# Masks of the exponentials for 54 later attention tiles: from VectorE's fused compare-and-multiply to a GpSimd addition and ScalarE's row sums

## The chip, the cores and the metric

One core of one Trainium2 chip. Its engines run their own instruction streams side by side and wait for each other through semaphores: TensorE (PE in the rows, its weight loads PEld), VectorE (DVE), ScalarE (ACT), GpSimd (POOL), and SyncE (SP), which here only issues DMAs. The metric is the device time of one execution in microseconds (us); lower is better.

## What is computed

Top-k attention, and behind it a mixture of experts with one expert a row. Eight batches of eight heads, 576 positions, 64 columns a head; every row of scores keeps its 32 largest values:

```python
scores = scale * np.matmul(q, k.transpose(0, 1, 3, 2))
kth = np.partition(scores, -top_k, axis=-1)[..., -top_k:-top_k + 1]
mask = scores >= kth
scores = np.where(mask, scores, -1000000000.0)
scores = scores - np.max(scores, axis=-1, keepdims=True)
attn = np.exp(scores)
attn = attn / (np.sum(attn, axis=-1, keepdims=True) + 1e-09)
return np.matmul(attn, v)
# then: x = rows of all heads side by side (4608 x 512), 8 experts
logits = x @ w_gate + modality_bias[modality_id]
e_idx = np.argmax(logits, axis=1)
h = np.maximum(x[mask] @ w1[e], 0.0)        # 512 -> 1024
out[mask] = gate_w[mask, None] * (h @ w2[e])  # 1024 -> 512
```

## The kernel before

The scores are cut into 288 tiles of 128 rows by 576 columns: nine for each of the 32 pairs of heads, 36 for each batch. One Python loop of 310 steps writes all engines' instructions; step i works on a different stage of each of about a dozen tiles, so that a tile u passes through the steps u-2 to u+9. The order inside a step is fixed by the code, except on VectorE, where `arrange` sorts the step's operations by given weights and puts the masking operation last.

What happens to tile u, with the step and the engine:

- u-2: the scores on PE (`qk`, L410) and their copy to SBUF on ACT (`sevac`, L420: tile `Ssb`, ten buffers).
- u, u+1: the largest values of six pieces of the row (`cand`, L427) and their merging (`mg`, L438 to L440) on DVE: the first 24 values.
- u+3: signs against the 24th value on ACT (`K`, L460). u+4: `y` = scores times signs on POOL (`pool_y`, L466), so that only the values under the 24th stay positive. u+5: the next eight of them on DVE (`find`, L470), and, at every third tile, the 32nd value `kth` of three tiles (`pick`, L477 to L479).
- u+6: the exponential of the whole tile on ACT (`expo`, L484: `ex`, three buffers). u+7: `keep` (L490) on DVE compares with `kth`, multiplies, writes `P` and sums the rows. u+8: `gate` (L562), one element of `P` read on POOL, which holds POOL until the masking is done.
- u+9: the transposes of `P` on PE (L577), their copy on ACT (L585, `PT`), and behind that the products with v (L605).

For tiles under 48 that are not the third of three there is another way, already in the kernel before (`early`; in the first batch without the tiles of `wide`, below): at u+7 `hide` (L497) on DVE writes -2^100 where a score is under `kth` and 0 elsewhere, in bf16; at u+8 `hidden` (L503) on POOL adds it to the scores (`z`, in a buffer of `ex`), and at the end of ACT's step u+8 `masked` (L558) takes the exponential of `z`, writes `P` and sums the rows in the same instruction. `expo`, `keep` and `gate` are then left out. Four of nine tiles under 36 go a third way (`wide`), which the change doesn't touch. The third tile of three (u % 3 = 2) always goes through `keep`.

Beside this the experts' products fill PE (`moe`, a queue of operations, L883 and L896; each of weight 0.88 is one product of 128x512 or two of 128x256). Every step gives PE a budget, `STEP` = 3.36, from which the attention's own costs are taken; what is left over, up to a cap, is spent on the queue. Results of the experts leave by indirect DMAs that POOL issues (L911, two for a slot of 256 rows), at most one in a step, behind `y`. What the queue still holds when the loop ends is done before the remaining slots, which are computed in three products each for precision (L1127, L1156, L1172). These names of the planner matter to the change: `side`, `rush`, `chore`, `posted` and `sends` hold the work of routing and of planning slots, `moe` the experts' operations.

Of the kernel before, what the change touches and what calls it, by code (L numbers as in the profile page):

```python
# [11 lines left out]
BF = mybir.dt.bfloat16  # L12
# [9 lines left out]
CAP = 2.6  # L22
# [8 lines left out]
STEP = 3.36  # L31
# [10 lines left out]
LR = LT + 2  # L42
LE = LR - 1
TL = LR + 2
# [21 lines left out]
END = (-3, 1.0)  # L66
SP_ = (0, 0, 0, 0, 0)
HUGE = float(2.0 ** 100)
EARLY = 48
WIDE = 36  # L70
BIG = float(2.0 ** 80)
MAX_TOP = 64.0
# [7 lines left out]
def kernel(  # L80
# [14 lines left out]
    B, H, S, D = q.shape  # L95
# [4 lines left out]
    NT = NPAIR * 9  # L100
# [111 lines left out]
    hT = const.tile([128, FC, SLOT], FT, name="hT")  # L212
# [31 lines left out]
    V.tensor_scalar(idw, idf, BIG * (1.0 + 2.0 ** -7), None, op0=OP.mult)  # L244
    tops = const.tile([128, WIDE], FT, name="tops")
    tiny = flat(w2b)[:, 2 * S + 448:2 * S + 576].bitcast(BF)
# [4 lines left out]
    zr = const.tile([128, XW], FT, name="zr")  # L251
# [123 lines left out]
    role = lambda i: (i - 1) % 9  # L375
    wide = lambda i: main[0] and i < WIDE and role(i) < 4

# [64 lines left out]
    def small(i0):  # L442
        on = main[0] and i0 < WIDE
        s = tops[:, i0:i0 + 3] if main[0] and i0 < WIDE else wk.tile([128, 3], FT, name="sm", bufs=6)
        for x in range(3):
            T[i0 + x]["s"] = s
        G.tensor_scalar(s, T[i0]["mg"][:, :, 0], -1.0, 0.0 if on else 1.0, op0=OP.mult, op1=OP.min if on else OP.mult)
# [33 lines left out]
    def expo(i):  # L481
        t = T[i]
        t["ex"] = wk.tile([128, S], FT, name="ex", bufs=XB)
        A.activation(t["ex"], t["S"], AF.Exp, bias=t["s"][:, i % 3:i % 3 + 1])  # L484
# [7 lines left out]
    def hide(i):  # L492

        t = T[i]
        x = 2 * (i % 2)
        t["hb"] = hT[:, x:x + 2, :].rearrange("p f t -> p (f t)").bitcast(BF)[:, :S]
        V.tensor_scalar(t["hb"], t["S"], kth[:, i:i + 1], -HUGE, op0=OP.is_lt, op1=OP.mult)  # L497

    def hidden(i):
# [229 lines left out]
    chore = deque()  # L729
# [214 lines left out]
    side = deque()  # L944
    rush = deque()
    moe = deque()
    sends = deque()
    puts = deque()
    posted = deque()
# [114 lines left out]
    def bounds():  # L1064
# [3 lines left out]
        V.tensor_scalar(bt, kth, KTH_MAX, 0.0, op0=OP.is_ge, op1=OP.add, accum_out=bd_[:, 1:2])  # L1068
        V.tensor_scalar(bt[:, :WIDE], tops, -MAX_TOP, 0.0, op0=OP.is_le, op1=OP.add, accum_out=bd_[:, 2:3])

    def beyond():

        bb = bd_.bitcast(BF)[:, 8:11]
        V.tensor_scalar(bb, bd_[:, 0:3], 0.0, None, op0=OP.is_gt)
        pbad = psX.tile([128, 3], FT, name="X")
        PE.matmul(pbad, onesb, bb, start=True, stop=True)
        V.tensor_reduce(bd_[:, 3:4], pbad, axis=AX.X, op=OP.add)
        V.tensor_copy(badi, bd_[0:1, 3:4])
# [16 lines left out]
            keep_warm(KP)  # L1095
        sevac(x)
    ok = lambda x: 0 <= x < NT
    early = lambda u: wide(u) or u < EARLY and u % 3 != 2
    dn_of = lambda u: den[(u // 36) % 2][:, (u // 9) % HP, role(u):role(u) + 1]
    PREP, PREP0 = dict(zip(PJ, "tkq")), dict(zip(PJ0, "tkq"))  # L1100
    two = lambda nm, shape: [wk.tile(shape, FR, name=nm + x) for x in "hl"]
# [88 lines left out]
    spare_pe = 0.0  # L1190
# [19 lines left out]
    for i in range(LAST):  # L1210
# [5 lines left out]
        cost = COST["trans"] * ok(i - TL)  # L1216
        p, j = divmod(i, 9)
        u = i - TL
# [14 lines left out]
        u = i - (KL + 1)  # L1233
# [4 lines left out]
        while after:  # L1238
            after.popleft()()
        u = i - LE  # L1240
        if ok(u) and not early(u):
            expo(u)
        while nxt:
# [3 lines left out]
        u = i - TL  # L1247
        if ok(u):
            evac(u)
        u = i - LR - 1  # L1250
# [59 lines left out]
        u = i - (TL + 1)  # L1310
        if avs:
            c, f = avs.popleft()
            f()
            cost += c
        if ok(u) and role(u) in (3, 7, 8):
            f = av(u // 9, role(u), xTs(u // 36)[(u // 9) % HP])
# [12 lines left out]
            bounds()  # L1329
        if i == NT + LR + 4:  # L1330
            beyond()
        spare_pe = min(spare_pe + (STEP if i < NT + TL + END[0] else END[1]) - cost, CAP)
        while seen[0] and spare_pe > 0:
            if i < NT + ME and not alone[0]:
                more_moe()
# [2 lines left out]
            c, f, new = moe[0]  # L1338
# [31 lines left out]
        for x in range((RNQ if quick else RN) if rush else 0):  # L1370
            f = rush.popleft() if rush else PAUSE
# [6 lines left out]
        for x in range((SNQ if quick else SN) - len(small_)):  # L1378
            f = side.popleft() if side and not rush else PAUSE
# [6 lines left out]
        if ok(i - LR):  # L1386
            u = i - LR
            end.append(Op("keep", lambda: hide_wide(u) if wide(u) else hide(u) if early(u) else keep(u, dn_of(u)), got, *cut_))
# [192 lines left out]
```

## Time and profile before

| | us |
|---|---|
| median of 3 runs (1189.47 to 1190.32) | 1189.72 |
| the profiled execution | 1187.03 |
| its span, first to last instruction | 1185.4 |
| busy in the span: PE, DVE | 1154.1, 1085.2 |
| busy in the span: ACT, POOL | 971.7, 662.2 |
| granted TensorE clock, mean | 0.993 |

The attention fills the span to about 1010 us, the slots in three products the rest. Busy times count an instruction from its start to its end; on PE and DVE instructions overlap in a pipeline, so that the distance between the starts of two neighbours says more of the pace than the length of one. In a list in order of time the columns are start, length, engine, line, operation, tiles written and read, and in brackets the idle time ahead of it with what ended it.

### The profile page before, as it was taken

The page shows a single profiled execution, that of the slowest core. Times are in us where ns is not written, and L with a number is a line of the kernel's source. Part 1 is how long each engine was busy: PE and PEld are TensorE (multiplying, and loading weights), DVE is VectorE, ACT ScalarE, POOL GpSimd, SP SyncE. Part 2 cuts the span into 40 slices and gives each one's busy share as a digit, 9 for nine tenths or more (in the row PEclk, how much of TensorE's full clock was granted, in tenths as well). Part 3 has the DMA queues.
Part 4 walks back from the last instruction along what each step waited for, and adds up shares of the span by engine and source line. Part 5 has one row for each costly group of instructions (what it writes and reads, how often), then busy time and mean ns, then how long its engine had stood idle before and what let it go on. Part 6 is the DMA issues. An engine that isn't in the chain of part 4 may idle for free.

```text
span 1185.4 us, 28210 instructions
## 1 busy us (share of the span) xinstructions
PE 1154.1 (97%) x7998; PEld 908.1 (77%) x7998; DVE 1085.2 (92%) x5473; ACT 971.7 (82%) x1995; POOL 662.2 (56%) x1281
## 2 busy tenths in 40 slices
PE   8999989999999999999999999999999999999998
PEld 6777768687777868778686878778687777589987
DVE  7999999999999999999999899999999998476762
ACT  5988969998999889998999899989999887355653
POOL 6888875565556465566656566557655655221111
PEclk9999989999999999999999999999999999999999
DMA  5664468653677367665786458564765554287750
GB/s 123 161 187 90 89 183 228 191 134 97 168 222 210 83 174 229 166 152 129 217 228 176 109 151 250 155 166 128 201 188 133 176 139 153 73 287 245 249 191 22
DMA packets 204325, 197.11 MB, mean 166 GB/s; under 512 B 104414, under 2 KB 151534, under 8 KB 204161
## 3 DMA queue, kind: packets, MB, share of 16 engines
q1 hardware_dynamic: 196880, 175.92, 54.6%
q0 software_dynamic: 6080, 19.00, 4.5%
q8 instruction: 67, 1.10, 0.4%
q14 instruction: 98, 0.79, 0.2%
q10 hardware_dynamic: 1200, 0.30, 0.1%
HBM read 118.63 MB, written 24.23 MB: 121 GB/s over the span
## 4 chain that ended last, share of the span: by engine, by line
PE 48%; DVE 43%; ACT 4%; issue 2%; POOL 1%; DMA 1%; SPq 0%; POOLq 0%; ACTq 0%; DVEq 0%
DVE cand L427 12%; PE E L883 8%; DVE mg L470 8%; PE E L896 8%; PE X L605 7%; DVE P L490 7%; PE S L410 5%; PE X L1172 5%; PE T L577 5%; PE X L1156 4%; DVE cand L438 2%; DVE cand L439 2%; DVE mg L440 2%; DVE mg L438 2%; PE E L1156 1%
## 5 line engine op out<-in xcount | busy, mean ns | idle before, releaser
L427 DVE MAX8 cand<-Ssb 128x8 f32<-128x96 f32 x1632 | 366.8, 244 | 1.4 <-ACT Ssb L420 1.4
L466 POOL TENSOR_TENSOR y<-Ssb,K 128x576 f32<-128x576 f32 x272 | 347.1, 1276 | 7.1 <-ACT K L460 6.8
L410 PE MATMUL S<-ks,qs 128*128 128x288 f32 x992 | 222.7, 346 | 8.2 <-ACT Ssb L420 5.1
L460 ACT ACTIVATE K<-Ssb,n 128x576 bf16<-128x576 f32 x272 | 216.6, 796 | 8.8 <-POOL y L466 8.4
L470 DVE MAX8 mg<-y 128x8 f32<-128x576 f32 x288 | 213.1, 740 | 3.9 <-POOL y L466 3.9
L420 ACT ACTIVATE Ssb<-S 128x576 f32<-128x576 f32 x270 | 178.2, 660 | 44.8 <-PE S L410 32.2
L883 PE MATMUL E<-xgT,w1b 128*128 128x256 f32 x832 | 201.4, 384 | 2.6 <-ACT hT L887 1.6
L585 ACT ACTIVATE PT<-T 128x640 f32<-128x640 f32 (+1 forms) x288 | 192.8, 669 | 11.3 <-PE T L577 6.9
L896 PE MATMUL E<-w2b,hT 128*128 128x512 f32 x416 | 195.9, 597 | 0.5 <-ACT hT L887 0.2
L410 PEld LDWEIGHTS S<-ks,qs 128*128 128x128 f32 x992 | 152.9, 190 | 53.8 <-issue 30.0
L484 ACT ACTIVATE ex<-Ssb,sm 128x576 f32<-128x576 f32 x244 | 193.4, 793 | 0.0
L490 DVE SCALAR_TENSOR_TENSOR P<-Ssb,kth,ex 128x576 f32<-128x576 f32 x226 | 185.8, 822 | 3.1 <-ACT ex L484 1.7
L883 PEld LDWEIGHTS E<-xgT,w1b 128*128 128x128 f32 x832 | 150.8, 190 | 29.3 <-ACT hT L887 6.8
L562 POOL TENSOR_SCALAR spare<-P 1x1 f32<-1x1 f32 x226 | 40.8, 180 | 217.1 <-DVE mg L438 180.4
L577 PE MATMUL T<-idf,P 128*128 128x128 f32 x1080 | 157.8, 273 | 1.3 <-ACT PT L585 0.7
L605 PE MATMUL X<-PT,vm 128*64 128x256 f32 (+1 forms) x1536 | 146.6, 333 | 1.0 <-ACT xgT L842 0.5
L577 PEld LDWEIGHTS T<-idf,P 128*128 128x128 f32 x1080 | 130.2, 141 | 4.0 <-ACT PT L585 1.9
L605 PEld LDWEIGHTS X<-PT,vm 128*64 128x64 f32 x1536 | 88.2, 137 | 45.7 <-issue 11.0
L896 PEld LDWEIGHTS E<-w2b,hT 128*128 128x128 f32 x416 | 72.7, 190 | 59.6 <-issue 55.0
L453 POOL TENSOR_SCALAR n<-mg 128x1 f32<-128x1 f32 x288 | 63.2, 219 | 97.2 <-DVE mg L440 80.2
L1178 POOL DMA_INDIRECT out_dram<-ot,tk x12 | 12.1, 1012 | 90.9 <-ACT ot L1177 90.9
L460 ACT ACTIVATION_READ_ACCUMULATOR K<-Ssb,n 128x1 f32 x272 | 59.9, 220 | 0.0
(273 smaller groups left out, 2253.2 us busy)
## 6 DMA issues: line engine op xcount, KB each, us to landing
w1b<-in_moe_w_dram SPq DMA_DIRECT2D x76, 512.0 KB
w2b<-in_moe_w_dram SPq DMA_DIRECT2D x76, 512.0 KB
ks<-st SPq DMA_DIRECT2D x62, 288.0 KB
ks<-st SPq DMA_DIRECT2D x62, 256.0 KB
qs<-st SPq DMA_DIRECT2D x124, 128.0 KB
xg<-xs SPq DMA_DIRECT2D x19, 516.0 KB
vm<-in_v_dram SPq DMA_DIRECT2D x32, 256.0 KB
km<-in_k_dram SPq DMA_DIRECT2D x63, 128.0 KB
```

What stands on the lines that cost most here:

```text
L410: PE.matmul(ps[:, hf, :288], l, m, start=(n == 0), stop=(n == len(terms) - 1))
L427: return [lambda s=s: V.max(c[:, s * 8:s * 8 + 8], T[i]["S"][:, bnd[s]:bnd[s + 1]]) for s in range(NSUB)]
L460: A.activation(t["K"], t["S"], AF.Sign, scale=2.0 ** -24 - 1.0, bias=t["n"][:, 1, i % 3:i % 3 + 1], accum_out=t["n"][:, 0, i % 3:i % 3 + 1])
L466: G.tensor_tensor(t["y"], t["S"], t["K"], op=OP.mult)
L470: V.max(t["mg"][:, i % 3, 24:32], t["y"])
L484: A.activation(t["ex"], t["S"], AF.Exp, bias=t["s"][:, i % 3:i % 3 + 1])
L490: V.scalar_tensor_tensor(t["P"], t["S"], kth[:, i:i + 1], t["ex"], op0=OP.is_ge, op1=OP.mult, accum_out=dn)
L577: PE.transpose(T[i]["pt"][:, x, :], (Pm if c == 4 else Pb[c % 2])[:, h * 512 + x * 128:h * 512 + x * 128 + 128], idf)
L585: A.activation(o, T[i]["pt"][:, :n], AF.Exp if wide(i) else AF.Copy)
L605: PE.matmul(o.rearrange("p (a b) -> p a b", a=2) if j < 8 else o, l, r, start=(c == 0), stop=(c == 4))
L883: PE.matmul(ps[:, f % 2], w1b[:, c, f * 128:(f + 1) * 128], xgT[:, c, :], start=(c == 0), stop=(c == KC - 1))
L896: PE.matmul(o["py"], hT[:, f, t * 128:(t + 1) * 128], w2b[:, f, :], start=(f == 0), stop=(f == FC - 1))
```

## The change

In the steps r = 15 to 32 of a batch's 36 (`CALM`, counted from the batch's end behind the pipeline), where none of the routing and planning queues holds work and the experts' queue holds 3 to 24 operations, a tile from 48 on that isn't the third of three goes the way of `hide`, `hidden` and `masked`. The tile's mask lies in `zr`, one buffer for all of them. In the step in which such a tile is masked the experts' budget is smaller by 0.22 (`DROP`).

```diff
+CALM = (15, 33)
+DROP = 0.22
...
-        t["hb"] = hT[:, x:x + 2, :].rearrange("p f t -> p (f t)").bitcast(BF)[:, :S]
+        if i < EARLY:
+            t["hb"] = hT[:, x:x + 2, :].rearrange("p f t -> p (f t)").bitcast(BF)[:, :S]
+        else:
+            t["hb"] = zr.bitcast(BF)[:, :S]
         V.tensor_scalar(t["hb"], t["S"], kth[:, i:i + 1], -HUGE, op0=OP.is_lt, op1=OP.mult)
...
-    early = lambda u: wide(u) or u < EARLY and u % 3 != 2
+    calm = set()
+    early = lambda u: wide(u) or u < EARLY and u % 3 != 2 or u in calm
...
         u = i - LE
+        if (ok(u) and u >= EARLY and u % 3 != 2 and CALM[0] <= (i - TL - 2) % 36 < CALM[1] and 3 <= len(moe) <= 24
+                and not any((side, rush, chore, posted, sends))):
+            calm.add(u)
         if ok(u) and not early(u):
             expo(u)
...
-        spare_pe = min(spare_pe + (STEP if i < NT + TL + END[0] else END[1]) - cost, CAP)
+        spare_pe = min(spare_pe + (STEP - DROP * (i - LR in calm) if i < NT + TL + END[0] else END[1]) - cost, CAP)
```

In the changed program GpSimd's addition stands 74 times where it stood 20 times: 54 tiles changed their way. Of them 23 pairs are the first and second tile of the same three, and 8 stand alone. Two pairs and one single lie in the attention's last 25 us.

GpSimd, in the third batch, from the end of one step to the middle of the third behind it. `sm` is the negated row maximum, `y` and `n` belong to the search of other tiles, `P_119` and `P_120` are the two buffers of masked tiles, `out_dram` is the indirect DMA of an expert's result. Before:

```order
L447 TENSOR_SCALAR sm<-mg 128x3
L562 TENSOR_SCALAR spare<-P_120 1x1
L466 TENSOR_TENSOR y<-Ssb,K 128x576
L453 TENSOR_SCALAR n<-mg 128x1
L562 TENSOR_SCALAR spare<-P_120 1x1
L466 TENSOR_TENSOR y<-Ssb,K 128x576
L453 TENSOR_SCALAR n<-mg 128x1
L562 TENSOR_SCALAR spare<-P_119 1x1
L466 TENSOR_TENSOR y<-Ssb,K 128x576
```

The same place now (lines of the changed kernel: L508 is `hidden`, L468 `y`, L916 the DMA):

```order
L449 TENSOR_SCALAR sm<-mg 128x3
L508 TENSOR_TENSOR ex<-Ssb,zr 128x576
L468 TENSOR_TENSOR y<-Ssb,K 128x576
L916 DMA out_dram<-ot,stok_130 4608x512
L627 MEMSET spare 1x1
L455 TENSOR_SCALAR n<-mg 128x1
L508 TENSOR_TENSOR ex<-Ssb,zr 128x576
L468 TENSOR_TENSOR y<-Ssb,K 128x576
L455 TENSOR_SCALAR n<-mg 128x1
L567 TENSOR_SCALAR spare<-P_119 1x1
L468 TENSOR_TENSOR y<-Ssb,K 128x576
```

In two of three steps a whole-tile addition stands ahead of `y` in place of the one-element `gate`; here one of the experts' DMAs has come between the two additions, as it does in four of the pairs. On VectorE only the masking instruction is another one (L502 `zr<-Ssb,kth` for L490 `P<-Ssb,kth,ex`), last in its step as before.

ScalarE, the same steps. Before:

```order
L484 ACTIVATE ex<-Ssb,sm 128x576
L420 ACTIVATE Ssb<-S 128x576
L585 ACTIVATE PT<-T 128x640
L318 ACTIVATE st<-X 128x512
L460 ACTIVATE K,n<-Ssb,n 128x576
L484 ACTIVATE ex<-Ssb,sm 128x576
L420 ACTIVATE Ssb<-S 128x576
```

Now:

```order
L486 ACTIVATE ex<-Ssb,sm 128x576
L422 ACTIVATE Ssb<-S 128x576
L590 ACTIVATE PT<-T 128x640
L563 ACTIVATE P_120,den_125<-ex,sm 128x576
L320 ACTIVATE st<-X 128x512
L462 ACTIVATE K,n<-Ssb,n 128x576
L422 ACTIVATE Ssb<-S 128x576
```

The exponential of a changed tile has left the place ahead of `Ssb` and stands two steps later behind `PT`, with the row sums (`den`) as a second output; the third tile of three keeps its place.

TensorE at the end of the attention. `X<-idf,xT` are the transposes of the last batch's rows, `w1b` and `w2b` the weights of the last slot of the queue, `xg` rows of the next slot. Before:

```order
L638 MATMUL X<-idf,xT 128x128 x4
L896 MATMUL E<-w2b,hT 128x512 x2
L638 MATMUL X<-idf,xT 128x128 x4
L896 MATMUL E<-w2b,hT 128x512
L638 MATMUL X<-idf,xT 64x128 x4
L868 MATMUL X<-idf,xg 128x128 x4
L896 MATMUL E<-w2b,hT 128x512 x7
L1127 MATMUL X<-idf,xg 128x128 x8
L896 MATMUL E<-w2b,hT 128x512
```

Now:

```order
L643 MATMUL X<-idf,xT 128x128 x4
L888 MATMUL E<-xgT,w1b 128x256 x2
L643 MATMUL X<-idf,xT 128x128 x4
L888 MATMUL E<-xgT,w1b 128x256 x4
L643 MATMUL X<-idf,xT 64x128 x4
L888 MATMUL E<-xgT,w1b 128x256 x4
L901 MATMUL E<-w2b,hT 128x512 x8
L901 MATMUL X<-w2b,hT 128x512 x3
L1133 MATMUL X<-idf,xg 128x128 x8
L901 MATMUL X<-w2b,hT 128x512 x5
```

From the first of these rows on, 11 products of 128x512 were left of the slot; now 16 of them and 10 of 128x256. (The four transposes of `xg` at L868 are gone from this place; `xgT` can't take the next slot's rows before the first layer is done.)

## Rows read from the trace of the kernel before

**Rows 1.** Busy us of each engine in two stretches, instructions in parentheses.

```profile
core 0: us, PE busy (x) PEld busy (x) DVE busy (x) ACT busy (x) POOL busy (x), PEclk, DMA share, GB/s
...
343.00:393.00 50.00, 49.24 (x308) 36.52 (x307) 49.97 (x269) 46.60 (x96) 29.71 (x61) 1.00 0.73 190
...
985.00:1010.00 25.00, 24.75 (x159) 18.15 (x157) 20.49 (x81) 18.21 (x35) 12.39 (x23) 1.00 0.51 167
```

**Rows 2.** VectorE in order of time, later batches: `find` and one `keep`.

```profile
370.06 0.74 DVE L470 MAX8 mg<-y 128x8 f32<-128x576 f32 x1
...
372.25 0.81 DVE L490 SCALAR_TENSOR_TENSOR P<-Ssb,kth,ex 128x576 f32<-128x576 f32 x1
...
373.10 0.75 DVE L470 MAX8 mg<-y 128x8 f32<-128x576 f32 x1
...
376.14 0.75 DVE L470 MAX8 mg<-y 128x8 f32<-128x576 f32 x1
...
379.61 0.74 DVE L470 MAX8 mg<-y 128x8 f32<-128x576 f32 x1
...
637.62 0.74 DVE L470 MAX8 mg<-y 128x8 f32<-128x576 f32 x1
...
647.05 0.74 DVE L470 MAX8 mg<-y 128x8 f32<-128x576 f32 x1
```

**Rows 3.** GpSimd in order of time, the second step of Rows 2.

```profile
373.37 1.28 POOL L466 TENSOR_TENSOR y<-Ssb,K 128x576 f32<-128x576 f32 x1
```

**Rows 4.** VectorE in order of time, tiles 36 to 39, the way now extended.

```profile
134.09 0.50 DVE L497 TENSOR_SCALAR hT<-Ssb,kth 128x576 bf16<-128x576 f32 x1
134.63 0.74 DVE L470 MAX8 mg<-y 128x8 f32<-128x576 f32 x1
...
136.82 0.70 DVE L497 TENSOR_SCALAR hT<-Ssb,kth 128x576 bf16<-128x576 f32 x1
137.56 0.74 DVE L470 MAX8 mg<-y 128x8 f32<-128x576 f32 x1
...
139.76 1.05 DVE L490 SCALAR_TENSOR_TENSOR P<-Ssb,kth,ex 128x576 f32<-128x576 f32 x1
...
140.86 0.74 DVE L470 MAX8 mg<-y 128x8 f32<-128x576 f32 x1
...
142.68 0.16 DVE L632 TENSOR_SCALAR rd<-den 128x36 f32<-128x36 f32 x1
...
143.43 0.35 DVE L630 RECIPROCAL rd<-rd 128x36 f32<-128x36 f32 x1
143.71 0.41 DVE L497 TENSOR_SCALAR hT<-Ssb,kth 128x576 bf16<-128x576 f32 x1
144.16 0.73 DVE L470 MAX8 mg<-y 128x8 f32<-128x576 f32 x1
```

**Rows 5.** GpSimd in order of time, the same steps as Rows 4.

```profile
134.68 1.29 POOL L503 TENSOR_TENSOR ex<-Ssb,hT 128x576 f32<-128x576 f32 x1 [0.61 <-DVE hT L497]
135.92 1.29 POOL L466 TENSOR_TENSOR y<-Ssb,K 128x576 f32<-128x576 f32 x1
...
137.67 1.28 POOL L503 TENSOR_TENSOR ex<-Ssb,hT 128x576 f32<-128x576 f32 x1
138.91 1.29 POOL L466 TENSOR_TENSOR y<-Ssb,K 128x576 f32<-128x576 f32 x1
```

**Rows 6.** GpSimd in order of time: one DMA of an expert's result.

```profile
365.33 1.06 POOL L911 DMA_INDIRECT out_dram<-ot,stok  x1 [0.17 <-issue]
...
366.57 0.19 POOL L453 TENSOR_SCALAR n<-mg 128x1 f32<-128x1 f32 x1
```

**Rows 7.** TensorE in order of time: the last slot of the queue.

```profile
1032.45 6.28 PE L896 MATMUL E<-w2b,hT 128*128 128x512 f32 x14
1038.56 1.04 PE L1127 MATMUL X<-idf,xg 128*128 128x128 f32 x8
```

**Rows 8.** ScalarE in order of time: the row sums of one `masked`.

```profile
137.80 0.20 ACT L558 ACTIVATION_READ_ACCUMULATOR Pm<-ex,sm 128x1 f32 x1
137.89 0.77 ACT L460 ACTIVATE K<-Ssb,n 128x576 bf16<-128x576 f32 x1
```

**Rows 9.** Who waited for `masked` (L558): us in all, times.

```profile
  PEld T L577: 4.2, 6
```

## The prediction

> **What bounds the kernel now.** I read three views: busy time by stretch, then VectorE in order of time, then GpSimd and TensorE at the same places. In the stretch from 343 to 393 us, most of which the change touches, VectorE is busy 49.97 of 50 us, ScalarE 46.60, GpSimd 29.71 [rows 1]. TensorE shows 49.24 there, but its lengths include the pipeline, so this alone doesn't say that it is full. The pace tells it: `find` opens each of VectorE's steps, and its starts lie 3.04, 3.04 and 3.47 us apart (370.06, 373.10, 376.14, 379.61), the long step being the one with the pick [rows 2]. Three steps take 9.55 us there and 9.43 us between 637.62 and 647.05 [rows 2]; I use 9.49. An engine that follows such a rhythm without a gap is the bound. VectorE is the bound of the calm steps, and a shorter VectorE step is worth its whole length there as long as nothing else takes over. From about 985 us on it is different: VectorE falls to 20.49 of 25 us while TensorE stays at 24.75 [rows 1]. Behind the attention TensorE goes on without a pause (14 products follow at 6.11 us, 0.436 each [rows 7]). There every product that is added lengthens the time.
>
> **What the change takes off VectorE.** In the trace of before one and the same way is already used for two of three tiles from 36 to 47, so its price can be read. From the start of the masking instruction to the next `find` it is 0.54 us with `hide` (134.09 to 134.63 [rows 4]) and 0.85 us with `keep` (372.25 to 373.10 [rows 2]). That is 0.31 us a tile. Of 54 tiles five lie in the last 25 us, where TensorE is the bound, and bring nothing. The other 49 would give 15.2 us, if nothing waited.
>
> **What it puts on GpSimd, and who waits for that.** Each tile adds one addition of 1.28 us and drops the short gate. Before, `y` started at 373.37, ended at 374.65 and was over 0.64 us ahead of the next mask (375.29 is the `keep` in whose step it ran: 3.04 behind 372.25 [rows 2, 3]). With an addition ahead of it `y` moves back by about 1.2 us and runs into the mask. The early rows show what happens then. The addition starts right behind the first mask, at 134.68, `y` follows from 135.92 to 137.21 [rows 5]; the second mask wants to start at 136.82 and takes 0.70 instead of 0.50 us [rows 4]. One step later `y` runs from 138.91 to 140.20 [rows 5], and the `keep` of the third tile, at 139.76, takes 1.05 instead of 0.81 us [rows 2, 4]. So masks of either kind wait for GpSimd's whole-tile products, 0.20 and 0.24 us here, and both waits stand on VectorE.
>
> Summed over three steps, the early rows have `find` at 134.63, 137.56, 140.86 and 144.16: 2.93, 3.30 and 3.30 us. The last step also holds a reciprocal of a batch's sums, 0.28 us (143.43 to 143.71) and about 0.07 for the addition ahead of it (L632; its neighbours' spacing); the mask behind the reciprocal was 0.09 us shorter than usual (0.41 against 0.50) [rows 4]. I take 0.35 off and put 0.09 on: 9.27 us against 9.49. **A pair gains 0.22 us of the 0.62 that it takes off.** 21 pairs lie ahead of the last 25 us: **-4.6 us**. The bounds are 0 (a pair's waits grow to its saving) and 0.62 (no waits): 0 to -13.0.
>
> A single tile gains 0.31 us once and makes one `keep` behind it wait 0.24: -0.07 each, seven of them: **-0.5 us**; bounds 0 and -2.2.
>
> **The DMAs between two additions.** In four pairs an expert's DMA stands behind the first addition's `y`. It holds GpSimd for 1.24 us (365.33 to 366.57 [rows 6]). In the early rows the second addition could start at 137.67, 0.15 us behind the end of its mask (137.52) [rows 4, 5]; with 1.24 us more ahead of it it starts some 1.1 us later, and its `y` would end at about 141.3 instead of 140.20. `find` wants that `y` at 140.86 [rows 4], and the `keep` in between contends with the addition or with `y`, whichever runs. Either way the next step starts 1.1 us late or more. Four times 1.1: **+4.4 us**. Bounds: 0, if the DMA is issued beside the wait for the mask, and 1.3 us each, +5.2; I take the value nearer to the rows' own arithmetic. A DMA in the step behind the second addition has the long step ahead of it and costs nothing; DMAs behind a single addition likewise.
>
> **The smaller budget.** 54 times 0.22 are 11.9 units, at 0.88 an operation some 13; by the program's order 10 or 11 operations end up behind the last steps of the attention (16 products of 128x512 and 10 half as wide, against 11). While VectorE is the bound, taking products out of TensorE's steps saves nothing. At the end, where TensorE is the bound, they cost 0.436 us each [rows 7]: 10.5 times 0.436, **+4.6 us**. Bounds: +4.4 and +4.8; a gap that they fill would take off 1 us at most.
>
> **Costed at nothing.** The row sums add 0.09 us to ScalarE (137.80 to 137.89 [rows 8]), 4.9 us over 54 tiles; they lie beside VectorE's steps, since ScalarE is busy 46.60 of 50 us [rows 1] and fifteen steps with ten changed tiles add 0.9. If that cover is gone, they cost up to 4.4 us for the 49. One mask buffer for all tiles: the first addition ends at 135.97, the second mask starts at 136.82 [rows 4, 5], 0.85 us of cover. `expo` moves two steps back on ScalarE, to a place right ahead of the transposes. In the early steps PE's weight loads waited for it six times, 4.2 us in all [rows 9], with no expert products in the queue. TensorE has spare time under VectorE's pace, so I charge nothing; the third rival prices it.
>
> **The sum**, against the profiled execution: 1187.03 - 4.6 - 0.5 + 4.4 + 4.6 = 1187.03 + 3.9 = 1190.9 us. The median of the runs is 1189.72, 2.7 us above that execution. On the median's scale the forecast is **1193.6 us**, slower by 0.33%. Its own range, by the bounds of the DMAs and 0.1 us a pair either way, is 1190.5 to 1196.
>
> **Rivals.** First, *the waits stay away*, and the time falls: the masks find GpSimd free, because steps with experts' work put `y` elsewhere than the early steps did. The full saving is 15.2 us against 4.6 of products: 1189.7 - 10.6 = 1179.1; with half of the waits and half of the DMAs' loss about 1186. For it: no calm pair exists in the trace. Against it: both engines' order inside a step is the same as early, and VectorE's step is the bound in both. It decides if the second mask's start lies behind the end of `y`, 0.4 us later than in the early rows.
>
> Second, *the DMAs cost nothing*, so that gain and deferred products cancel: 1189.72 - 4.6 - 0.5 + 4.6 = 1189.2, no change that can be measured. For it: GpSimd's queue was idle ahead of most small instructions before. Against: with an addition in the step it isn't.
>
> Third, *ScalarE and TensorE take over*: the late exponential holds the transposes, the copies behind them, and by the scores' buffers the next tiles. By the early rows 0.7 us a time at most (4.2 over 6 [rows 9]); if 0.1 us of that reaches VectorE for each of 49 tiles, +4.9: 1198.5. For it: ScalarE is at 93% before and gets 0.09 a tile. Against: scores run two steps ahead.
>
> Fourth, *a mask waits for all that is left of `y`*. In the early rows 0.39 us were left when the second mask started and 0.44 at the `keep` [rows 4, 5], the waits were 0.20 and 0.24; in full they would cost 0.39 more a pair, 8.2 for 21: 1201.8. The rows show it otherwise, so it gets little. The Trainium skill, "SBUF — State Buffer", section "Who interferes with whom", says that VectorE and GpSimd hold a shared pair of ports as an exclusive lock, so that the second one fully blocks until the first has finished. The trace agrees that one waits for the other; the wait that it shows is about 0.2 us shorter than what was left.
>
> **How the numbers follow.** Forecast 0.50, of which 0.10 may land inside 0.2%; waits stay away 0.20 (half of it near 1186, the rest lower); DMAs free 0.18; ScalarE and TensorE 0.10; full waits 0.02. About 0.2%, 2.4 us, is what a measurement of this kernel can tell from no change: 1187.3 to 1192.1. Slower: 0.40 + 0.10 + 0.02 = 0.52. Same: 0.10 + 0.18 = 0.28. Faster: 0.20. The range must leave out at most 0.2: from 1185.5, in the middle of the first rival, to 1198.5, the third; below lie 0.1, above some 0.07.
>
> **What would show it.** In the changed profile: `hide` in calm steps at about 0.50 us for the first of a pair and 0.70 for the second, the third tile's `keep` at 1.05; three steps at 9.27; a `find` that waits for `y` about 1 us where a DMA stands between two additions; 74 additions of 1.28 us; a longer stretch of `w2b` products ahead of the first three-product slot, by some 4.6 us. Masks of 0.50 and 0.81 throughout would make the first rival right, gaps on VectorE that end with a ScalarE instruction the third.

## The result

| | before | after |
|---|---|---|
| median of 4 runs, us | 1189.60 (1188.76 to 1190.32) | 1204.48 (1202.79 to 1205.50) |
| ratio, 95% interval | | 1.0128 (1.0116 to 1.0141) |
| the profiled execution, us | 1187.03 | 1205.50 |
| its span | 1185.4 | 1203.8 |
| from the `find` of tile 59 to that of tile 287 | 793.31 | 799.31 |
| from the last product with v to the first product of a three-product slot | 19.31 | 28.75 |

The change makes the kernel 14.9 us slower. The forecast was 1193.6, in a range from 1185.5 to 1198.5; direction right, size not. Of the 18.5 us between the two profiled executions 3.0 arise ahead of the first changed tile (the same program there took between 0 and 3.4 us more in other executions, so these belong to the execution), 6.0 in the stretch that holds nearly all changed tiles, and 9.4 behind the attention.

The long stretch first, from tile 59's `find` to tile 287's. The columns are length, then busy us (and instructions) of PE, PEld, DVE, ACT, POOL, then granted clock, DMA share, GB/s. Before:

```profile
209.72:1003.03 793.31, 787.21 (x5326) 604.59 (x5324) 777.72 (x4135) 708.46 (x1471) 476.17 (x939) 1.00 0.61 167
```

After:

```profile
212.69:1012.00 799.31, 783.55 (x5287) 598.15 (x5286) 780.70 (x4074) 710.74 (x1517) 544.42 (x938) 1.00 0.60 163
```

Read the idle time, not the busy time: before, TensorE (first figure) paused 6.1 us in 793, VectorE (third) 15.6. TensorE had the least to spare. Most of VectorE's idle time is itself a wait for TensorE, in the routing steps (us in all, times, longest):

```profile
DVE lt L667 <- PE X L659: 11.9, 6, 3.0
```

Lengths on TensorE include the pipeline, so this alone settles nothing; e2 and e10 below do. After, with some 40 records fewer TensorE pauses 15.8 us. GpSimd is busy 68 us more.

A pair of changed tiles did what the prediction's early rows said. VectorE after, in order of time (start, length; answers to [rows 4]):

```profile
353.37 0.50 DVE L502 TENSOR_SCALAR zr<-Ssb,kth 128x576 bf16<-128x576 f32 x1
...
353.91 0.73 DVE L472 MAX8 mg<-y 128x8 f32<-128x576 f32 x1
...
356.11 0.69 DVE L502 TENSOR_SCALAR zr<-Ssb,kth 128x576 bf16<-128x576 f32 x1
...
356.84 0.74 DVE L472 MAX8 mg<-y 128x8 f32<-128x576 f32 x1
...
359.03 1.04 DVE L492 SCALAR_TENSOR_TENSOR P<-Ssb,kth,ex 128x576 f32<-128x576 f32 x1
...
360.12 0.73 DVE L472 MAX8 mg<-y 128x8 f32<-128x576 f32 x1
```

Masks of 0.50 and 0.69, a `keep` of 1.04, steps of 2.93 and 3.28 us: 0.50, 0.70, 1.05, 2.93 and 3.30 were forecast.

So did the four DMAs between two additions. GpSimd at one of them (answers to [rows 5, 6]):

```profile
375.77 1.10 POOL L916 DMA_INDIRECT out_dram<-ot,stok  x1 [0.15 <-issue]
...
377.33 1.29 POOL L508 TENSOR_TENSOR ex<-Ssb,zr 128x576 f32<-128x576 f32 x1
378.58 1.79 POOL L468 TENSOR_TENSOR y<-Ssb,K 128x576 f32<-128x576 f32 x1
```

and VectorE beside it, a `keep` and the `find` behind it:

```profile
378.28 0.96 DVE L492 SCALAR_TENSOR_TENSOR P<-Ssb,kth,ex 128x576 f32<-128x576 f32 x1
...
380.41 0.76 DVE L472 MAX8 mg<-y 128x8 f32<-128x576 f32 x1 [1.04 <-POOL y L468]
```

That wait of 1.04 us stands at all four places (380.41, 519.17, 732.67, 876.77).

What was not forecast shows where a DMA stands behind the *second* addition. GpSimd, then VectorE:

```profile
526.47 1.29 POOL L468 TENSOR_TENSOR y<-Ssb,K 128x576 f32<-128x576 f32 x1
527.91 1.38 POOL L916 DMA_INDIRECT out_dram<-ot,stok  x1 [0.15 <-issue]
...
529.88 1.27 POOL L468 TENSOR_TENSOR y<-Ssb,K 128x576 f32<-128x576 f32 x1
```

```profile
530.03 1.18 DVE L479 TENSOR_TENSOR eq<-i9s,n 128x27 f32<-128x27 f32 x1
```

The pick's first instruction, 27 columns wide, takes 1.18 us where it takes 0.16 to 0.27 in 88 of the 96 picks of before: the next `y` runs from 529.88 to 531.15 and the pick's instruction ends with it. The prediction had let this DMA cost nothing, because the long step follows; but the long step is long because of the pick, and the pick waits for GpSimd too. The price stood in the trace of before, where eight picks take 0.69 to 1.09 us, one of them beside a `y` that runs from 423.56 to 424.83:

```profile
423.80 1.08 DVE L477 TENSOR_TENSOR eq<-i9s,n 128x27 f32<-128x27 f32 x1
```

In the attention's last 25 us VectorE after:

```profile
1002.84 0.76 DVE L472 MAX8 mg<-y 128x8 f32<-128x576 f32 x1 [1.16 <-POOL y L468]
...
1007.33 1.52 DVE L502 TENSOR_SCALAR zr<-Ssb,kth 128x576 bf16<-128x576 f32 x1 [1.02 <-POOL ex L508]
...
1012.00 0.76 DVE L472 MAX8 mg<-y 128x8 f32<-128x576 f32 x1 [1.16 <-POOL y L468]
```

The attention's last four steps take 2.34, 3.40, 2.06 and 2.20 us before, and an addition with its `y` holds GpSimd for 2.5: `find` waits for `y`, and a mask waits until the one mask buffer has been read.

The end, TensorE after (answers to [rows 7]):

```profile
1044.04 7.13 PE L901 MATMUL E<-w2b,hT 128*128 128x512 f32 x16 [0.69 <-ACT hT L892]
1051.01 2.74 PE L901 MATMUL X<-w2b,hT 128*128 128x512 f32 x6
...
1054.46 4.46 PE L901 MATMUL X<-w2b,hT 128*128 128x512 f32 x10
```

These are 32 records of 128x512 behind the attention, and 32 of 128x256 ahead of them, against 28 and none. At 0.436 us for a wide record and half of that for a narrow one they take 8.7 us more (an estimate), and TensorE waits 0.69 us for `hT`; the whole end is 9.44 us longer. The program's order counts a product once; a trace counts two records for it. The prediction took the 10.5 products from the order and the 0.436 us from the trace, half of a product's price.

### The profile page after: what moved, and what is told of

It reads as the page before. It is cut to its first block, busy times and chain, and to the rows that moved or that the text cites. A ratio compares the mean times of both kernels' runs of the same rounds, so it can differ in the third digit from the quotient of the medians.

```text
span 1203.8 us, 28079 instructions
## 1 busy us (share of the span) xinstructions
PE 1159.6 (96%) x7994; PEld 908.9 (75%) x7994; DVE 1091.8 (91%) x5419; ACT 976.3 (81%) x2048; POOL 730.3 (61%) x1281
## 4 chain that ended last, share of the span: by engine, by line
PE 58%; DVE 29%; ACT 8%; issue 2%; POOL 2%; DMA 0%; POOLq 0%; ACTq 0%; DVEq 0%
PE E L901 10%; PE E L888 10%; PE X L610 9%; DVE cand L429 8%; PE S L412 7%; PE T L582 6%; DVE mg L472 5%; PE X L1178 5%; PE X L1162 4%; DVE P L492 3%; ACT K L462 2%; DVE cand L440 2%; DVE cand L441 2%; ACT Ssb L422 1%; PE E L1162 1%
## 5 line engine op out<-in xcount | busy, mean ns | idle before, releaser
L468 POOL TENSOR_TENSOR y<-Ssb,K 128x576 f32<-128x576 f32 x272 | 350.3, 1288 | 11.3 <-ACT K L462 10.9
L412 PE MATMUL S<-ks,qs 128*128 128x288 f32 x992 | 222.3, 346 | 9.0 <-ACT Ssb L422 6.2
L412 PEld LDWEIGHTS S<-ks,qs 128*128 128x128 f32 x992 | 152.9, 190 | 54.4 <-issue 29.1
L901 PE MATMUL E<-w2b,hT 128*128 128x512 f32 x400 | 187.6, 597 | 3.8 <-ACT ot L911 2.0
L492 DVE SCALAR_TENSOR_TENSOR P<-Ssb,kth,ex 128x576 f32<-128x576 f32 x182 | 157.7, 867 | 0.9 <-ACT ex L486 0.9
L486 ACT ACTIVATE ex<-Ssb,sm 128x576 f32<-128x576 f32 x190 | 150.6, 793 | 0.6 <-DVE P L492 0.6
L455 POOL TENSOR_SCALAR n<-mg 128x1 f32<-128x1 f32 x288 | 70.1, 244 | 89.0 <-DVE mg L442 68.3
L567 POOL TENSOR_SCALAR spare<-P 1x1 f32<-1x1 f32 x182 | 32.9, 181 | 145.7 <-DVE mg L440 120.4
L901 PEld LDWEIGHTS E<-w2b,hT 128*128 128x128 f32 x400 | 70.2, 190 | 63.1 <-issue 55.7
L508 POOL TENSOR_TENSOR ex<-Ssb,zr 128x576 f32<-128x576 f32 x54 | 69.3, 1284 | 20.4 <-DVE zr L502 16.5
L1184 POOL DMA_INDIRECT out_dram<-ot,tk x12 | 11.9, 988 | 93.3 <-ACT ot L1183 93.3
```

Of the source, the lines that this page charges most:

```text
L412: PE.matmul(ps[:, hf, :288], l, m, start=(n == 0), stop=(n == len(terms) - 1))
L468: G.tensor_tensor(t["y"], t["S"], t["K"], op=OP.mult)
L492: V.scalar_tensor_tensor(t["P"], t["S"], kth[:, i:i + 1], t["ex"], op0=OP.is_ge, op1=OP.mult, accum_out=dn)
L901: PE.matmul(o["py"], hT[:, f, t * 128:(t + 1) * 128], w2b[:, f, :], start=(f == 0), stop=(f == FC - 1))
```

## Experiments

Ratios are to the kernel before on the same chip, with 95% intervals; e1 to e16 are names of runs.

| run | median us | ratio |
|---|---|---|
| e2_budget | 1193.46 | 1.0047 (1.0030 to 1.0064) |
| e1_drop0 | 1203.58 | 1.0126 (1.0109 to 1.0143) |
| e5_hold | 1205.38 | 1.0141 (1.0124 to 1.0158) |
| e6_drop0_hold | 1204.60 | 1.0136 (1.0113 to 1.0159) |
| e7_clean | 1197.79 | 1.0089 (1.0074 to 1.0103) |
| e8_beside | 1192.59 | 1.0039 (1.0026 to 1.0052) |
| e9_end | 1194.56 | 1.0054 (1.0039 to 1.0069) |
| e4_y_twice | 1205.59 (one run) | |
| e10_short_keep | 1190.53 | 1.0007 (0.9997 to 1.0017) |
| e12_short_budget | 2257.58 | 1.8993 (1.8959 to 1.9026) |
| e14_short_budget2 | 1194.59 | 1.0048 (1.0034 to 1.0061) |
| e13_pool_alone | 1207.87 | 1.0151 (1.0135 to 1.0167) |
| e11_masked_first | 1200.22 | 1.0089 (1.0073 to 1.0106) |
| e15_first_drop0 | 1199.23 | 1.0088 (1.0075 to 1.0102) |
| e16_clean_first | 1196.92 | 1.0067 (1.0055 to 1.0080) |

### The budget, alone and taken back

e2: the kernel before with the smaller budget in the same 54 steps, and no tile on the new way (written as an edit of the changed kernel).

```diff
-    early = lambda u: wide(u) or u < EARLY and u % 3 != 2 or u in calm
+    early = lambda u: wide(u) or u < EARLY and u % 3 != 2
```

> The kernel before with the smaller budget alone, in the same 54 steps; no tile changes its way. Theory A: the end is longer by 11 operations of 0.87 us, 9.4 us: 1199.0 us, and VectorE's steps are as before. Theory B (the products cost 0.44 us each, as the prediction had it): 1194.2. Theory C (the budget costs nothing by itself): 1189.6.

Measured 1193.46, 4.9 us over before (by the ratio 3.6 to 7.6). That is theory B's sum, the prediction's, but its parts are other ones. The end is longer by 9.44 us, to the hundredth as in the changed kernel, but the loop is shorter:

```profile
212.51:998.84 786.33, 776.72 (x5281) 596.81 (x5280) 777.54 (x4126) 706.68 (x1467) 472.63 (x937) 1.00 0.61 165
```

The stretch is 7.0 us shorter than before (786.33 against 793.31) though no step of VectorE lost any work: taking 10.5 us off TensorE (787.21 to 776.72) shortened the loop by two thirds of it. The prediction held that this saves nothing "while VectorE is the bound". Since e2 has the planner's steps of the changed kernel, product by product, the two are best compared with each other: same end, and the new way costs 13.0 us in the stretch (799.31 against 786.33), 10 us by the ratios.

e1: the changed kernel with the budget of before.

```diff
-DROP = 0.22
+DROP = 0.0
```

> The changed kernel with DROP = 0: TensorE's budget as before. Theory A (the experts' products that the smaller budget left for the end cost 0.87 us each, 9.4 us in all, and the rest of the loss is VectorE waiting for a GpSimd that is late behind the experts' DMAs): the end behind the attention is back at the length of before, 19.3 us from the last attention product to the first three-product slot, against 28.7 in the changed kernel. With another budget 51 tiles change their way and the DMAs fall elsewhere: none between two additions, five behind a second addition ahead of the attention's last 25 us. 20 pairs at -0.25 us and five DMAs at +1.0: 1189.6 us, 1188 to 1192. Theory B (the end is late for another reason, the smaller budget costs 4.6 us at most): 1199 to 1202.

The end is back at 19.31 us, as theory A said, and yet the kernel takes 1203.58. With a full budget the new way costs 15 us instead of 10. Theory A, which had 1188 to 1192, missed. Giving TensorE its work back made the new way dearer; that fits no theory in which VectorE's waits are the whole loss.

### Keeping the DMAs away from the additions

```diff
-        elif puts and puts[0][0] <= 0:
+        elif puts and puts[0][0] <= 0 and i - 1 - LR not in calm:
```

> The changed kernel, but an expert's DMA is not issued in a step that holds an addition; it waits for the next step without one, two steps at most. Theory A (GpSimd's DMA of 1.24 us beside an addition pushes y into the find, the pick or the keep behind it): four waits of find of 1.04 us go, three waits of the pick's first instruction of 1.0 us, about 1.2 us at single tiles and their neighbours: 1196 us, 1194 to 1198. Theory B (the DMAs cost the same wherever they stand): 1204.5.

> The changed kernel with DROP = 0 and with the experts' DMAs kept out of steps that hold an addition. Theory A: both losses go and the pairs' gain is left: 20 pairs at -0.25 us, the waits of pick gone: 1184.6 us, 1183 to 1187. Theory B (the additions themselves cost more than they give): 1190 or more.

Theory A missed both times, theory B was right: 1205.38 and 1204.60, no better than without. The four waits of `find` went, others came; in e6, too, steps 70, 109, 151, 187, 210 and 226 are 0.5 to 1.0 us shorter than in e1 and others are longer. GpSimd and VectorE in e5, where a held DMA leaves one step later:

```profile
384.16 1.07 POOL L916 DMA_INDIRECT out_dram<-ot,stok  x1 [0.28 <-POOL qbd L368]
...
385.86 1.28 POOL L508 TENSOR_TENSOR ex<-Ssb,zr 128x576 f32<-128x576 f32 x1
```

```profile
387.18 1.53 DVE L502 TENSOR_SCALAR zr<-Ssb,kth 128x576 bf16<-128x576 f32 x1 [1.51 <-POOL ex L508]
```

Now the DMA delays the *first* addition of the next pair, and the second mask waits 1.51 us for the mask buffer: the cover of 0.85 us that the prediction gave the single buffer is gone. In a run of pairs such a DMA found no step in which it was free.

### Which of the tiles cost

With DROP = 0 the planner does the same in each step as before, so the tiles can be split: 13 pairs with no DMA in their three steps (e7), 7 pairs with one and 4 singles (e8), the last 7 tiles (e9).

```diff
+MASKS = (64, 65, 70, 71, 100, 101, ...)
...
-        if (ok(u) and u >= EARLY and u % 3 != 2 and CALM[0] <= (i - TL - 2) % 36 < CALM[1] and 3 <= len(moe) <= 24
-                and not any((side, rush, chore, posted, sends))):
+        if i + 1 in MASKS:
             calm.add(u)
```

> TensorE's budget as before (DROP = 0), and only 13 pairs change their way: those in whose three steps no expert's DMA is issued, all ahead of the attention's last 40 us. The planner's products and DMAs stand step by step as in the run with DROP = 0. Theory A (a pair gains 0.25 us on VectorE; the loss comes from what else GpSimd has to do beside the additions): 13 times 0.25 less: 1186.4 against 1189.6, or a ratio of 0.9973. Theory B (the late exponential couples ScalarE and TensorE, whatever GpSimd does): slower than before by 1 to 4 us, with VectorE waiting for ScalarE behind runs of pairs.

> The complement of the clean pairs, ahead of 960 us: 7 pairs with an expert's DMA in one of their three steps, and 4 single tiles; budget as before. Theory A: the pairs' -1.8 us, five DMAs behind a second addition that push y into the pick at +1.0, one planning step at +1.0, four second masks at +0.45: 1189.6 + 6.0 = 1195.6. Theory B (DMAs don't matter): 1187.8, or for the coupling of ScalarE and TensorE the same per tile as in the run of the clean pairs.

> Only the seven tiles masked from 966 us on change their way, three pairs and one single; budget as before. The prediction has them bring nothing and cost nothing. Theory A (in the last 25 us TensorE is the bound and its transposes wait for the exponential that now comes at the end of ScalarE's step): the attention ends 4 us later and the end behind it is 2.7 us longer, as in the run with DROP = 0: 1196. Theory B (the end is hidden): 1189.6.

The expectations start from 1189.6, the kernel before on this chip took 1187.59, so read the differences. e8 costs 5.0 us (4.6 by the ratio) where theory A had 6.0, and by the spacing of `find` five steps of the pick are longer by 1.02 to 1.03 us (steps 70, 109, 151, 187, 226) and a planning step by 0.99, as it said. e9 costs 7.0 (6.4 by the ratio) where theory A had 6.4; but the end behind the attention, which was to be longer, is 19.31 us there, so its loss is all inside the attention. **e7 missed by most**: the clean pairs cost 10 us. In seven of the 13 pairs the three steps are shorter by 0.20 to 0.25 us; the other six are between 0.02 us shorter and 0.39 longer. All 13 together are 0.35 us shorter, while the stretch is 9.5 us longer (802.80): the loss lies behind the pairs. Steps 111 to 114, behind the masks of steps 109 and 110, take 3.91, 4.26, 4.28 and 3.51 us against 3.04, 3.47, 3.04 and 3.04 before. In three of them `keep` waits for ScalarE's exponential, which is theory B's mechanism at more than twice its size:

```profile
378.06 0.82 DVE L493 SCALAR_TENSOR_TENSOR P<-Ssb,kth,ex 128x576 f32<-128x576 f32 x1 [0.78 <-ACT ex L487]
...
381.85 1.28 DVE L493 SCALAR_TENSOR_TENSOR P<-Ssb,kth,ex 128x576 f32<-128x576 f32 x1 [0.37 <-ACT ex L487]
...
386.60 0.82 DVE L493 SCALAR_TENSOR_TENSOR P<-Ssb,kth,ex 128x576 f32<-128x576 f32 x1 [1.14 <-ACT ex L487]
```

How such a delay can start is seen at an earlier pair. ScalarE in e7:

```profile
341.63 0.65 ACT L423 ACTIVATE Ssb<-S 128x576 f32<-128x576 f32 x1 [1.42 <-DVE cand L441]
...
347.40 0.78 ACT L564 ACTIVATE P<-ex,sm 128x576 f32<-128x576 f32 x1
...
348.64 0.78 ACT L463 ACTIVATE K<-Ssb,n 128x576 bf16<-128x576 f32 x1
...
349.40 0.60 ACT L893 ACTIVATE hT<-E 128x512 f32<-128x512 f32 x1
```

and TensorE:

```profile
350.05 1.98 PE L902 MATMUL E<-w2b,hT 128*128 128x512 f32 x4 [0.63 <-ACT hT L893]
```

At 340.2 ScalarE has nothing to do for 1.42 us; the exponential used to stand there. It is done at 347.40, 0.76 us to the start of the next instruction, ahead of `K` and of the experts' copy `hT`, for which TensorE then waits 0.63 us. TensorE's lag grows: the copies of the transposes come 1.31 us behind `find` in step 96 of e7 and 8.02 us in step 112; before it was 1.33 and 5.16. That waits like the one shown make up the whole of it is not shown: with the exponential early in its step (e16, below) the lag in step 112 is 8.01 us.

### Is it the lock?

e4: the kernel before, with `y` computed twice in 40 steps of the pick.

```diff
+TWICE = (15, 33)
...
             pool_y(i - LY)
+            if TWICE[0] <= (i - TL - 2) % 36 < TWICE[1] and i >= 60 and (i - LT) % 3 == 2:
+                G.tensor_tensor(T[i - LY]["y"], T[i - LY]["S"], T[i - LY]["K"], op=OP.mult)
```

> The kernel before, no tile changes its way; in 40 of the steps that hold the pick, GpSimd computes the same y a second time right behind the first, so that a whole-tile product runs when the pick's first instruction wants to start. No DMA is moved. Theory A (the pick's instruction with two inputs waits until GpSimd's product has ended): it takes 1.0 to 1.3 us instead of 0.17 in those 40 steps, +40 us: about 1230. Theory B (the pick was late for the DMA's own sake): 1189 to 1192, the pick's instruction at 0.17.

A single run, 1205.59: the kind of wait is theory A's, its price not (about 1230). GpSimd's second `y` (L1402) and VectorE:

```profile
373.17 1.28 POOL L1402 TENSOR_TENSOR y<-Ssb,K 128x576 f32<-128x576 f32 x1
```

```profile
373.46 1.03 DVE L479 TENSOR_TENSOR jk<-eq,mg 128x27 f32<-128x27 f32 x1
```

It is the pick's second instruction that waits (0.17 to 1.03, ending with GpSimd's at 374.45), in 40 steps some 32 us in all; no DMA was moved. So a small instruction with two inputs does wait for GpSimd's product. But 32 us of waits lengthened the kernel by 18 (1187.59 before, on that chip): the rest found room in VectorE's idle time, as far as one run tells.

### Is VectorE the bound at all?

e10: the kernel before, the mask over half the columns in the 51 steps of e1; the other half is left out, so it says something of time and nothing of values.

```diff
+SHORT = (64, 65, 67, 68, 70, 71, 100, ...)
...
-        V.scalar_tensor_tensor(t["P"], t["S"], kth[:, i:i + 1], t["ex"], op0=OP.is_ge, op1=OP.mult, accum_out=dn)
+        w = S // 2 if i + LR in SHORT else S
+        V.scalar_tensor_tensor(t["P"][:, :w], t["S"][:, :w], kth[:, i:i + 1], t["ex"][:, :w], op0=OP.is_ge, op1=OP.mult, accum_out=dn)
```

> The kernel before; in the 51 steps of the run with DROP = 0 the masking instruction handles only the first 288 of a tile's 576 columns, so that VectorE's step is about 0.3 us shorter, as with the new way, and GpSimd, ScalarE and TensorE have what they had (the masks' other half is left out). Theory T (TensorE is the bound all through the attention: between the find of tile 59 and that of tile 287 its instructions fill 781 of 793 us, and VectorE's rhythm only hides that): 1186 to 1189, a gain of 3 us at most. The prediction's premise (VectorE is the bound of these steps): 45 tiles at 0.3 us, 1176.

**1190.53, ratio 1.0007 (0.9997 to 1.0017): 0.3 us less in each of 51 steps are worth nothing.** Not even the 3 us that theory T allowed came. The end behind the attention is 19.31 us as before, so the stretch decides:

```profile
210.96:1004.09 793.13, 786.19 (x5318) 603.21 (x5317) 770.22 (x4137) 708.03 (x1469) 479.11 (x939) 1.00 0.61 167
```

VectorE is busy 7.5 us less and idle 7.3 us more (15 us less in the masks, and some of it again in longer picks); TensorE fills the stretch as before. Each step is shorter by 0.30, and after a few of them VectorE stands still. VectorE in e10 behind steps 106 to 110:

```profile
371.38 0.50 DVE L492 SCALAR_TENSOR_TENSOR P<-Ssb,kth,ex 128x288 f32<-128x288 f32 x1
...
375.14 0.82 DVE L492 SCALAR_TENSOR_TENSOR P<-Ssb,kth,ex 128x576 f32<-128x576 f32 x1 [0.94 <-ACT ex L485]
```

That exponential started at 374.34 because ScalarE had waited for TensorE's products:

```profile
373.64 0.38 ACT L610 ACTIVATE xT<-X 128x256 f32<-128x256 f32 x1 [0.73 <-PE X L607]
374.22 0.22 ACT L610 ACTIVATE xT<-X 128x64 f32<-128x64 f32 x1 [0.20 <-PE X L607]
374.34 0.77 ACT L485 ACTIVATE ex<-Ssb,sm 128x576 f32<-128x576 f32 x1
```

This is the step of the prediction that failed first: VectorE sets the rhythm of the calm steps, but TensorE hardly pauses and only lags behind.

e12 joined the half mask with the smaller budget, in the 54 steps of the change.

> The same half mask in the 54 steps of the changed kernel, with its smaller budget; no tile changes its way, part of the masks is left out. To be read against the run with the smaller budget alone (1193.5). Theory T: with 9 us fewer products in TensorE's loop a shorter VectorE step is worth something, at most those 9 us less the 7 that the loop has given already, and the end stays 9.4 us longer: 1190 to 1193. The prediction's premise: 49 tiles at 0.3 us: 1179.

It took 2257.58 us and says nothing: with those masks the program did all the experts' products a second time at its end. e14 is the same with the masks of e10.

> The smaller budget of the changed kernel (in its 54 steps) with the half masks of the run of the short masks (in its 51 steps, the masks' other half left out), no tile changes its way. To be read against the smaller budget alone (1193.5, ratio 1.0047). Theory T (TensorE was the bound of the loop, so that VectorE's time becomes worth something once TensorE has 9 us less to do): VectorE waits 6.8 us there in place of 13.2, so 3 to 7 of the 13.8 us come through: 1187 to 1191. Theory T2 (the shorter step is given back in any case): 1193 to 1195. The prediction's premise: 1180.

1194.59, ratio 1.0048 against 1.0047 with the budget alone: theory T, by which 3 to 7 us should have come through, missed, and T2 was right. The stretch in e14:

```profile
209.74:996.00 786.26, 776.51 (x5280) 596.53 (x5279) 767.24 (x4126) 706.85 (x1467) 477.03 (x937) 1.00 0.61 165
```

It is as long as in e2 (786.33) with TensorE as busy as there (776.72); VectorE's idle time went from 8.8 to 19.0. Why it stays so is not shown; a reading that fits is that TensorE, which pauses 9.8 us there, was the bound even with ten us less work.

### GpSimd alone

e13: `y` twice in the 51 steps that hold an addition in e1, nothing else moved.

```diff
+ADDS = (64, 65, 67, 68, 70, 71, 100, ...)
...
             pool_y(i - LY)
+            if i - 1 in ADDS:
+                G.tensor_tensor(T[i - LY]["y"], T[i - LY]["S"], T[i - LY]["K"], op=OP.mult)
```

> The kernel before; in the 51 steps that hold an addition in the run with DROP = 0 GpSimd computes y twice, so that it is busy 1.28 us longer there, and VectorE, ScalarE and TensorE have what they had. Theory T: masks, picks and finds wait for a late GpSimd (0.24 us a mask, 1.0 us where an expert's DMA stands beside it), and about half of it reaches the end: 1193 to 1197. Rival (GpSimd's load alone costs nothing, the loss is the late exponential's): 1189 to 1190.

1207.87, more than theory T's 1193 to 1197. The stretch, and below it ScalarE's largest wait for GpSimd in it (us in all, times, longest):

```profile
209.79:1024.09 814.30, 792.25 (x5333) 606.45 (x5332) 809.45 (x4135) 712.86 (x1473) 556.46 (x989) 1.00 0.60 163
```

```profile
ACT K L461 <- POOL y L1402: 21.5, 24, 3.0
```

VectorE is busy 31.7 us more, its idle time falls to 4.9, so here it *is* the bound, and TensorE pauses 22. Shorter VectorE steps bring nothing, longer ones cost: neither engine had much room before. Besides the locks, a late `y` holds the buffers of `K`, and ScalarE waits for those.

### The place of the exponential

e11: the changed kernel, but `masked` stands where the exponential stood, ahead of the copy of the scores.

```diff
         if ok(u) and not early(u):
             expo(u)
+        if i - LR - 1 in calm:
+            masked(i - LR - 1, dn_of(i - LR - 1))
...
-        if ok(u) and early(u) and not wide(u):
+        if ok(u) and early(u) and not wide(u) and u not in calm:
```

> The changed kernel, but the masked exponential stands on ScalarE where the exponential stood before, ahead of the copy of the scores, instead of at the step's end. TensorE's transposes then have it 1.2 us sooner. Theory T: their waits, 5.6 us of TensorE's time between the finds of tiles 59 and 287, go, and where nothing takes their place the time falls by as much: 1199 to 1201. Rival (the scores' copies are now as late as the transposes' data were): 1204 or more.

1200.22, 4.3 us less than the changed kernel (4.6 by the ratios), as theory T said. In the changed kernel TensorE's weight loads wait for `masked` like this, in the stretch:

```profile
PEld T L582 <- ACT P L563: 5.3, 11, 0.8
```

In e11 none of these waits is left, and a part comes back as waits for the copies of the scores, as the rival said: the weight loads of the scores (L412) wait 13.4 us for `Ssb` in e11, 6.3 in the changed kernel.

> DROP = 0 and the masked exponential ahead of the copy of the scores. To be read against the run with DROP = 0 (1203.6, ratio 1.0126). Theory T (the place of the exponential and the budget are separate costs): 4 to 7 us less than with DROP = 0, 1197 to 1200, slower than before by what the late GpSimd costs. Rival (with the whole budget TensorE is late anyway and the place doesn't matter): 1203.

> The 13 pairs without a DMA beside them, budget as before, and the masked exponential ahead of the copy of the scores: what is left of the change when its three known costs are taken out. To be read against the run of the clean pairs (1197.8, ratio 1.0089). Theory T (VectorE's time is worth nothing while TensorE is the bound, each addition makes GpSimd late): 1192 to 1196, still slower than before. A version that beats the kernel before would be at 1187 or less.

e15 took 1199.23, 4.4 us under e1 (4.5 by the ratios): the place of the exponential costs as much with either budget. e16, the clean pairs with the exponential early, took 1196.92, below e7 by 0.2% and still 0.7% slower than before; theory T's range was just missed. No version with the new way beat the kernel before; e10 says that the time it takes off VectorE was worth nothing there.

## Why the prediction was wrong

**The bound** is the step that failed. The prediction set TensorE's 49.24 of 50 us aside ("its lengths include the pipeline, so this alone doesn't say that it is full") and took VectorE's even rhythm as proof. An engine can keep an even rhythm while another falls behind it, as long as buffers last. The trace of before shows TensorE falling behind. VectorE's `find` of one step, and `find` 16 steps later:

```profile
325.39 0.74 DVE L470 MAX8 mg<-y 128x8 f32<-128x576 f32 x1
...
376.14 0.75 DVE L470 MAX8 mg<-y 128x8 f32<-128x576 f32 x1
```

ScalarE's copies of the transposes that the program writes into the same two steps:

```profile
326.72 0.70 ACT L585 ACTIVATE PT<-T 128x640 f32<-128x640 f32 x1
...
381.30 0.76 ACT L585 ACTIVATE PT<-T 128x640 f32<-128x640 f32 x1
```

1.33 us behind `find`, then 5.16: TensorE loses 3.8 us on VectorE in 16 steps and makes it good in the long routing steps, where VectorE waits for it (11.9 us in the six of them). So the 15.2 us that the change takes off VectorE had no value (e10, e14), while waits put on TensorE through ScalarE did count (e11, e15).

**The gain of a pair**, -0.22 us, was measured as 0.20 to 0.25 in three steps that nothing else disturbs (seven of e7's 13 pairs), by the very waits of 0.20 and 0.24. It is right and worthless: e7 gives more than that back behind the pairs.

**DMAs between two additions**, +1.1 each: a wait of 1.04 at all four. **DMAs behind the second addition or behind a single tile**, costed at nothing: +1.0 wherever `y` then meets the pick or a planning step (e8, five and one), a price that the picks of before already paid at 423.80.

**The deferred products**, +4.6: the whole edit measures +4.9 (e2), but this is 9.44 at the end less some 7 in the loop (7.0 between the two profiled executions). The 14 in [rows 7] are records, that is seven products. So the term was mis-sized by a factor of two and the counter-term was set to zero; the two errors cancelled, so that its agreement with e2 is luck.

**The last five tiles** "bring nothing": the seven tiles of the last 45 us cost 6 to 7 us alone (e9).

**Costed at nothing**: the exponential's new place measures 4.3 us (e11; 4.6 by the ratios). The third rival named this mechanism and nearly its size, 4.9, and got a chance of 0.10, since "TensorE has spare time under VectorE's pace". The single buffer was free in pairs and not at the end (1.02 us) nor behind a late DMA (1.51 in e5).

**The fourth rival**, full waits, is wrong for the masks (0.19 and 0.23 us in the pair shown) and nearly right for the small instructions: at 530.03 there were 1.12 us left of `y` and the pick took 1.01 longer than its 0.17; at 373.46 in e4 0.99 were left and it took 0.86 longer. The Trainium skill, "SBUF — State Buffer", section "Who interferes with whom", says that a VectorE instruction with two SBUF inputs contends with a GpSimd instruction that reads SBUF, and that one with at most one SBUF input, outside the two-port performance modes, does not. The traces agree on the first, and on the second for `find`, which with one input keeps its 0.75 us beside a running `y` (373.10 in [rows 2], `y` from 373.37 in [rows 3]). The mask of the new way has one tile as input and does wait, 0.69 us for 0.50; whether it runs in such a mode no run here shows.

The sum, by runs, each good to some 2 us: 14.9 = 4.9 (budget, e2) + 4.3 (exponential, e11) + 5.7 for the rest, which no run isolates: by e8 and e13 the late GpSimd is in it, less whatever of VectorE's saving came through. Against the forecast of +3.9, the gain of 5.1 that was not there and the exponential alone are 9.4 of the 11 us that are missing. The parts don't add up freely: GpSimd's load alone cost 18 us where VectorE kept its long masks (e13), and e7, e8 and e9 together give more than e1. Why the 13 clean pairs still cost 8 us with the exponential early (e16) is left open between the late `y` and the later exponential.

**The range** failed because its upper end took one error at a time. Its parts all rested on one premise, and when that fell several moved together: no gain, a dearer exponential, dearer DMAs.

## What to carry to other kernels

An engine with an even rhythm is not yet the bound: compare the idle time of all engines over a long stretch, and look whether another engine's distance to it grows. To learn what a shorter instruction is worth, shorten it alone and measure, before building the way that shortens it. Count instructions and durations in the same unit, and where an operation is moved, look for what the engine does in the place it leaves.

## What the hardware showed

- A VectorE instruction of 27 columns with two inputs takes 0.17 us alone and 1.03 to 1.18 beside GpSimd's whole-tile product: it waits for nearly all that is left (0.86 of 0.99 us, 1.01 of 1.12). The position of small instructions counted here more than that of the masks (0.19 and 0.23).
- GpSimd's own product stretches beside a VectorE instruction with two inputs: `y` took 1.79 instead of 1.28 us (378.58) where a `keep` had been running since 378.28.
- Two engines can both be near their limit: 0.3 us less on VectorE in 51 steps changed nothing (e10), 31.7 us more of VectorE's busy time, by waits for GpSimd in as many steps, came with 18 us (e13).
